# An attention and bilinear FFN kernel: the first FFN step with four a-parts ahead of four b-parts

## The chip, the cores and the metric

One core of a Trainium2 chip runs the program. The metric is the device time of one execution in microseconds (us). The span in a profile, from the first to the last instruction, is about 1.8 us less.

## The reference, cut to what matters

```
q, k, v: (4, 8, 768, 64) fp32;  w_a, w_b: (512, 1536);  w_out: (1536, 512)
x   = lightning attention(q, k, v, lam)     # blockwise, with a decayed state, as (3072, 512)
out = ((x @ w_a) * (x @ w_b)) @ w_out       # (3072, 512) fp32
```

## The kernel before

The kernel works on 24 units of 128 rows. The first four are prepared at once, and the FFN is then done in groups of units with the attention of later units hidden between its matmuls. The first group runs its FFN while the weights are still coming in: w_a and w_b arrive as six chunks each of 256 columns (512 KB in fp32) and are cast to bf16, a0 on GpSimd, b0 and the other w_a chunks on VectorE, the other w_b chunks on ScalarE. A chunk feeds two "parts" of 128 columns with four matmuls each (the very first part is done in two cuts of rows, so it has eight). I call the chunks a0, b0, a1, b1 and so on.

```
pending = []                                  # order of the weight loads
for c in range(len(W_CHUNKS)):
    pending += [("a", c), ("b", c)]
...
# ffn(), first group
for c, w in enumerate(W_CHUNKS):
    fs = range(w_off[c] // 128, w_off[c + 1] // 128)
    a_sbs = [a_part(f, ...) for f in fs]      # 4 matmuls; ScalarE copies the result out
    if c + 1 < len(W_CHUNKS):
        cast_w("a", c + 1, "dve")
    for f, a_sb in zip(fs, a_sbs):
        b_part(f, xT, gt, a_sb, ab)           # 4 matmuls; VectorE multiplies a by b
        hook(f)                               # f = 0: state of unit 3, kvd matmuls + a state copy
    if c + 1 < len(W_CHUNKS):
        cast_w("b", c + 1, "act")
...
cast_w("a", 0, "pool")                        # ahead of the FFN
cast_w("b", 0, "dve")
```

## Time and profile before

| | before |
|---|---|
| median of the three runs first given | 233.59 us (233.25 to 234.13) |
| span of the profiled execution (a further one, which took 234.34 us) | 232.6 us |
| TensorE busy | 96% |
| longest TensorE wait after 18 us | 0.79 us, for the cast of a1 |

A timeline line reads: start, length, engine, source line, operation, output and inputs, count, and in brackets the idle time before it with what ended it. Some matmul records are missing from a trace, so x11 can stand for twelve. A cast that waited for a transfer starts 0.02 to 0.05 us after the transfer has landed in these traces, so its start serves as the landing.

### The profile page before, as it was taken

What the parts mean: (1) busy time and instruction counts of PE and PEld (TensorE: products, weight loads), DVE (VectorE), ACT (ScalarE), POOL (GpSimd) and SP (SyncE); (2) the same over time, 40 slices, a digit from 0 to 9 for tenths busy, and PEclk for the clock granted to TensorE, in tenths of its full rate; (3) what the DMA queues carried; (4) which work ended last, traced back from release to release, by engine and by line L of the source; (5) the groups of instructions that cost most, each with busy time, mean ns of one, the idle gap of its engine ahead of it and who ended that gap; (6) DMA issues with size and microseconds to landing.
All of it is one profiled execution on the core that took longest, in us unless ns stands there. A gap on an engine that the chain in (4) does not pass through costs nothing.

```text
span 232.6 us, 4506 instructions
## 1 busy us (share of the span) xinstructions
PE 223.8 (96%) x1756; PEld 124.8 (54%) x1779; DVE 116.4 (50%) x204; ACT 91.0 (39%) x172; POOL 50.4 (22%) x65
## 2 busy tenths in 40 slices
PE   7798999999999999999999999999999999999994
PEld 2574444449698654454544454544454544444493
DVE  1894666646479745684335474235483323332050
ACT  3683764056564342332233332333332333332261
POOL 6061000245655243333300543000300000000000
PEclk9999999999999999999999999999999999999999
DMA  4999999999999999999959997229300220000311
GB/s 150 300 264 351 348 361 298 268 209 193 204 223 164 214 188 221 217 171 205 333 192 206 213 181 129 93 92 202 69 3 0 90 93 0 1 0 10 128 45 48
DMA packets 96453, 38.84 MB, mean 167 GB/s; under 512 B 83376, under 2 KB 91952, under 8 KB 96432
## 3 DMA queue, kind: packets, MB, share of 16 engines
q1 hardware_dynamic: 96288, 38.54, 72.8%
q8 instruction: 14, 0.23, 0.4%
q14 instruction: 7, 0.06, 0.1%
q10 hardware_dynamic: 144, 0.00, 0.0%
HBM read 28.32 MB, written 6.29 MB: 149 GB/s over the span
## 4 chain that ended last, share of the span: by engine, by line
PE 87%; DMA 6%; SPq 3%; ACT 1%; issue 1%; DVE 0%
PE a_ps L434 26%; PE b_ps L434 26%; PE op L467 26%; DMA wst<-in_moe_w_a_dram 4%; SPq L128 3%; PE kq L308 2%; PE o_ps L350 2%; DMA q<-in_q_dram 2%; PE o_ps L340 2%; PE kvd L364 1%; PE tps L294 1%; SPq L149 1%; ACT o_kept L458 1%; DVE wa_sb L164 0%; PE kvd L385 0%
## 5 line engine op out<-in xcount | busy, mean ns | idle before, releaser
L447 DVE TENSOR_TENSOR ab<-a_sb,b_ps 128x512 bf16<-128x512 bf16 (+2 forms) x96 | 52.5, 552 | 76.7 <-PE b_ps L434 55.2
L434 PE MATMUL a_ps<-xT,wa_sb 128*128 128x512 bf16 (+3 forms) x378 | 76.5, 323 | 1.7 <-DVE wa_sb L164 0.8
L434 PE MATMUL b_ps<-xT,wb_sb 128*128 128x512 bf16 (+2 forms) x383 | 77.0, 326 | 0.1
L442 ACT CAST a_sb<-a_ps 128x512 bf16<-128x512 f32 (+2 forms) x96 | 45.5, 481 | 61.5 <-PE a_ps L434 58.1
L467 PE MATMUL op<-wo_sb,ab 128*128 128x512 bf16 (+2 forms) x300 | 64.2, 362 | 0.8 <-issue 0.3
L434 PEld LDWEIGHTS <-wb_sb 128*128 128x128 bf16 x384 | 34.4, 98 | 28.9 <-ACT wb_sb L159 0.5
L434 PEld LDWEIGHTS <-wa_sb 128*128 128x128 bf16 x388 | 33.9, 98 | 29.6 <-DVE wa_sb L164 1.3
L467 PEld LDWEIGHTS <-ab 128*128 128x128 bf16 x312 | 28.8, 98 | 29.9
L325 DVE TENSOR_TENSOR m<-kq,lotri 128x512 bf16<-128x512 f32 x47 | 29.3, 682 | 17.2 <-PE kq L308 17.1
L257 POOL TENSOR_TENSOR qk<-kf,lp_k 128x512 bf16<-128x512 f32 x18 | 19.0, 1056 | 75.1 <-PE a_ps L434 38.1
L262 POOL TENSOR_TENSOR qk<-qf,lp_q 128x512 bf16<-128x512 f32 x20 | 21.8, 1092 | 24.1 <-DMA qf<-in_q_dram 24.1
L462 ACT COPY o_sb<-op 128x512 f32<-128x512 f32 (+2 forms) x19 | 10.3, 541 | 34.0 <-PE op L467 34.0
L357 ACT CAST xT<-o_ps 128x512 bf16<-128x512 f32 x22 | 12.0, 590 | 18.1 <-PE o_ps L350 17.5
L396 DVE TENSOR_TENSOR st<-kvd,bdiag 128x512 bf16<-128x512 f32 x18 | 12.3, 683 | 3.9 <-PE kvd L364 3.2
L271 DVE CAST vb<-vf 128x512 bf16<-128x512 f32 x17 | 9.5, 560 | 0.0
L296 ACT COPY qkT<-tps 128x1024 bf16<-128x1024 bf16 x5 | 5.1, 1012 | 9.9 <-PE tps L294 9.9
L197 PE MATMUL idle<-idle_sb 128*128 128x128 bf16 (+1 forms) x31 | 7.1, 371 | 1.3 <-DVE idle_sb L192 1.3
L350 PE MATMUL o_ps<-m,vb 128*64 128x128 bf16 x192 | 7.9, 222 | 0.0
L271 POOL CAST vb<-vf 128x512 bf16<-128x512 f32 x7 | 4.4, 631 | 13.6 <-DMA vf<-in_v_dram 13.6
L159 ACT CAST wb_sb<-wst 128x1024 bf16<-128x1024 f32 x5 | 5.2, 1046 | 4.7 <-DMA wst<-in_moe_w_b_dram 4.7
L340 PEld LDWEIGHTS <-st 128*128 128x128 bf16 x80 | 5.4, 98 | 2.8
L308 PE MATMUL kq<-qkT 64*128 64x128 bf16 x160 | 6.6, 218 | 0.0
(57 smaller groups left out, 87.4 us busy)
## 6 DMA issues: line engine op xcount, KB each, us to landing
vf<-in_v_dram SPq DMA_DIRECT2D x24, 256.0 KB, 4.9
qf<-in_q_dram SPq DMA_DIRECT2D x20, 256.0 KB, 4.6
kf<-in_k_dram SPq DMA_DIRECT2D x20, 256.0 KB, 4.7
out_dram<-o_sb SPq DMA_DIRECT2D x16, 256.0 KB, 2.0
wst<-in_moe_w_a_dram SPq DMA_DIRECT2D x6, 512.0 KB, 8.8
wst<-in_moe_w_b_dram SPq DMA_DIRECT2D x6, 512.0 KB, 8.8
wst<-in_moe_w_out_dram SPq DMA_DIRECT2D x6, 512.0 KB, 8.6
out_dram<-o_kept SPq DMA_DIRECT2D x7, 256.0 KB, 2.8
```

Source lines behind the costliest of these rows:

```text
L257: eng_of(eng).tensor_mul(qk[:, 1], raw.pop((u, "k")), lp_k[:, u % NB].to_broadcast([128, H, D]))
L262: eng_of(eng).tensor_mul(U[u]["qk"][:, 0], raw.pop((u, "q")), lp_q[:, u % NB].to_broadcast([128, H, D]))
L271: eng_of(eng).tensor_copy(vb, vf)
L308: nc.tensor.matmul(kq[i][:, hp, :], lhsT=d["kT"][p, hp, :], rhs=d["qT"][p, hp, :], start=True, stop=True, skip_group_check=True)
L325: nc.vector.tensor_mul(m, kq[i], lotri_bc)
L350: nc.tensor.matmul(d["o"][p, hp, :], lhsT=d["vb"][:, 2 * hp + i, :], rhs=d["m"](i, hp), start=(first and hp == 0), stop=True, skip_group_c ...
L357: nc.scalar.copy(xT[:, :, col:col + BLK], o_ps)
L396: nc.vector.tensor_mul(st[:].rearrange("p hp i d -> p hp (i d)"), ps[:].rearrange("p hp i d -> p hp (i d)"), bdiag_bc)
L434: nc.tensor.matmul(ps[:, lo:hi], lhsT=w_sb[:, s, f * 128:(f + 1) * 128], rhs=xT[:, s, lo:hi], start=(s == 0), stop=(s == KS - 1), skip_gro ...
L442: nc.scalar.copy(a_sb[:, :gt], ps[:, :gt])
L447: nc.vector.tensor_mul(ab[:, f, :gt], a_sb[:, :gt], ps[:, :gt])
L467: nc.tensor.matmul(op[:, lo:hi], lhsT=ab[:, f, t * 128:(t + 1) * 128], rhs=wo_sb[:, f, lo:hi], start=(f == 0), stop=(f == FC - 1))
```

## The change

The intent is to give TensorE two blocks of a-parts while the first w_b chunk is still on its way: the loads become a0, a1, b0, b1, a2, ..., and the first step does four a-parts and then four b-parts.

```diff
+W_STEPS = ((0, 1), (2,), (3,), (4,), (5,))
-    a_pool = ctx.enter_context(tc.tile_pool(name="a", bufs=3))
+    a_pool = ctx.enter_context(tc.tile_pool(name="a", bufs=5))
-    for c in range(len(W_CHUNKS)):
-        pending += [("a", c), ("b", c)]
+    for cs in W_STEPS:
+        pending += [("a", c) for c in cs] + [("b", c) for c in cs]
...
-            for c, w in enumerate(W_CHUNKS):
-                fs = range(w_off[c] // 128, w_off[c + 1] // 128)
+            for i, cs in enumerate(W_STEPS):
+                nxt = W_STEPS[i + 1][0] if i + 1 < len(W_STEPS) else None
+                fs = range(w_off[cs[0]] // 128, w_off[cs[-1] + 1] // 128)
                 a_sbs = [a_part(...) for f in fs]
-                if c + 1 < len(W_CHUNKS):
-                    cast_w("a", c + 1, "dve")
-                for f, a_sb in zip(fs, a_sbs):
+                if i == 0:
+                    cast_w("b", cs[1], "act")
+                elif nxt:
+                    cast_w("a", nxt, "dve")
+                for n_f, (f, a_sb) in enumerate(zip(fs, a_sbs)):
                     b_part(f, xT, gt, a_sb, ab)
                     hook(f)
-                if c + 1 < len(W_CHUNKS):
-                    cast_w("b", c + 1, "act")
+                    if i == 0 and n_f == 1:
+                        cast_w("a", nxt, "dve")
+                if nxt:
+                    cast_w("b", nxt, "act")
...
+    cast_w("a", 1, "dve")
     cast_w("b", 0, "dve")
```

## The prediction

> **What bounds the kernel now.** I read the page's busy shares first, then the waits of TensorE, then the timeline of the stretch that the change touches.
>
> From the page, the totals and the head of the chain that ended last:
>
> ```profile
> PE 223.8 (96%) x1756; PEld 124.8 (54%) x1779; DVE 116.4 (50%) x204; ACT 91.0 (39%) x172; POOL 50.4 (22%) x65
> ...
> PE 87%; DMA 6%; SPq 3%; ACT 1%; issue 1%; DVE 0%
> ```
>
> TensorE is busy 223.8 of 232.6 us, and the chain that sets the end is TensorE for 87% of the span. A change of order that leaves the matmuls alone can gain only what TensorE waits. All its waits are these (engine, line, what it waited for, us in total, times, longest):
>
> ```profile
> PE idle L197 <- DVE idle_sb L192: 1.3, 1, 1.3
> PE tk L541 <- DVE scratch L532: 1.0, 2, 0.8
> PE a_ps L434 <- DVE wa_sb L164: 0.8, 1, 0.8
> PE a_ps L434 <- ACT xT L357: 0.4, 2, 0.2
> ```
>
> The third line is the one in reach of this change: 0.8 us, once, before the second w_a chunk. Here is where it comes from, in the timelines of TensorE and VectorE from 18 to 28 us (start, length, engine, line, operation, count, idle time before):
>
> ```profile
> 18.16 1.90 PE L434 MATMUL a_ps<-xT,wa_sb 128*128 128x384 bf16 x11 [0.23 <-ACT xT L357]
> 19.90 1.03 PE L434 MATMUL b_ps<-xT,wb_sb 128*128 128x512 bf16 x4
> 20.76 0.39 PE L364 MATMUL kvd<-vb,scratch 128*128 128x128 bf16 x4
> 20.98 1.03 PE L434 MATMUL b_ps<-xT,wb_sb 128*128 128x512 bf16 x4
> 22.80 1.90 PE L434 MATMUL a_ps<-xT,wa_sb 128*128 128x512 bf16 x8 [0.79 <-DVE wa_sb L164]
> 24.66 1.90 PE L434 MATMUL b_ps<-xT,wb_sb 128*128 128x512 bf16 x8
> 26.40 1.89 PE L434 MATMUL a_ps<-xT,wa_sb 128*128 128x512 bf16 x8
> ```
>
> ```profile
> 19.12 0.69 DVE L164 CAST wb_sb<-wst 128x1024 bf16<-128x1024 f32 x1 [0.68 <-DMA wst<-in_moe_w_b_dram]
> 22.05 0.69 DVE L164 CAST wa_sb<-wst 128x1024 bf16<-128x1024 f32 x1 [2.23 <-DMA wst<-in_moe_w_a_dram]
> 22.66 0.68 DVE L447 TENSOR_TENSOR ab<-a_sb,b_ps 128x512 bf16<-128x512 bf16 x1
> 23.25 0.68 DVE L396 TENSOR_TENSOR st<-kvd,bdiag 128x512 bf16<-128x512 f32 x1
> 23.85 0.68 DVE L447 TENSOR_TENSOR ab<-a_sb,b_ps 128x512 bf16<-128x512 bf16 x1
> 25.06 0.69 DVE L164 CAST wa_sb<-wst 128x1024 bf16<-128x1024 f32 x1 [0.53 <-DMA wst<-in_moe_w_a_dram]
> ```
>
> ```profile
> 23.56 1.04 ACT L159 CAST wb_sb<-wst 128x1024 bf16<-128x1024 f32 x1 [2.88 <-DMA wst<-in_moe_w_b_dram]
> ```
>
> Call the 512 KB weight chunks a0, b0, a1, b1, a2 and so on. Where a cast's engine sat idle until a transfer, the cast's start is the landing. The second chunk in the queue landed at 19.12 us, the third at 22.05, the fourth at 23.56, the fifth at 25.06: a step of 2.9 us and from then on 1.5 us each. TensorE needs 1.73 us for a chunk (24.66 to 26.40 is 1.74; eight matmuls of 0.216). So TensorE runs dry once, at the third chunk, and the supply stays ahead afterwards. Everything after 26.4 us is TensorE at full rate.
>
> **What the Trainium skill says.** "DMA: Bandwidth & Descriptors", section "Why a DMA increments its semaphore by 16 and not by 1": a transfer counts as landed only when each of the engines that share it has finished. That fits a third chunk 2.9 us behind the second although the windows view has 351 GB/s moving from 17.9 to 22.8 us, at which 512 KB take 1.5 us: the rest was later chunks in flight. "TensorE: Matmul & The Clock Gate", section "Part 1: The HAM clock gate (the "warmup" mystery)": the array falls to half clock after an idle window of about 3.4 us. The wait here is 0.79 us and the granted clock is 1.00 from 17.9 to 52.4 us, which agrees. The same part calls VectorE and ScalarE strict FIFOs; the order of casts, products and evacuations on each engine is therefore that of the program, and the trace shows them so.
>
> **The change, part by part.** I compared the programs of the two kernels on each engine.
>
> 1. *What stays.* TensorE has 3560 rows in both, VectorE 145, and after the first two chunks of the first FFN step the order is the same. No work is removed.
>
> 2. *Transfers.* The queue becomes a0, a1, b0, b1, a2, ...: only the second and third chunk swap. Both are 128x1024 fp32, so I let the landings stay with the place in the queue: a1 at 19.12, b0 at 22.05, b1 at 23.56, a2 at 25.06.
>
> 3. *TensorE up to the third chunk.* a0 runs as before. a1 is cast by VectorE from 19.12 to 19.81 (0.69) and starts at about 19.9, where b0 started. It takes 1.73 us, to 21.6. Then b0 is wanted: landing 22.05, VectorE cast 0.69, and the start at 22.80, exactly where a1 started before. Two chunks' work is available before the third lands, in either order; the order of the names doesn't change that. The wait grows from 0.79 to about 1.2 us, because piece V of unit 3 (the four kvd matmuls, 0.22 us, from 20.76 to 20.98) hangs on the first b-part and has left this gap.
>
> 4. *From 22.80 on.* b0 now carries the kvd matmuls: 1.73 + 0.22 = 1.95, so b1 could start at 24.75. Its cast on ScalarE is ready at 23.56 + 1.04 = 24.60. Before, TensorE was ready at 22.80 + 1.73 = 24.53 and started b1 at 24.66, so 0.13 us of waiting was paid there and now isn't. Net: 24.75 against 24.66, +0.09 us.
>
> 5. *VectorE before a2.* The a2 cast now stands behind the first two products and the state copy. First product: its fourth matmul starts at 22.80 + 3 x 0.216 = 23.45, lasts 0.38, and a product follows its last matmul by 0.11 (26.67 against 24.66 + 1.90): 23.94. With starts 0.60 apart when queued (22.66, 23.25, 23.85): state copy 24.54, second product 25.14, a2 cast about 25.76 to 26.45. From a cast's end to a matmul is 0.06 (22.74 to 22.80), so a2 can start at 26.51; TensorE is ready at 24.75 + 1.73 = 26.48. Before, a2 started at 26.40. The cast's slack of 0.65 us is used up, but only just: +0.11 us in all.
>
> 6. *Buffers.* Eight parts are in hand, not four. The PSUM bank of a part is asked for again seven parts later, some 6 us on, and a_sb gets five buffers; neither makes a new wait. The b2 cast (landing 26.56, ready 27.60) is wanted at 28.2 as before.
>
> Sum: 0.22 (kvd matmuls moved onto the path) - 0.13 (wait for b1 gone) + 0.02 (wait for the a2 cast) = +0.11 us. All that follows is TensorE at full rate and is shifted by it: 233.59 + 0.11 = 233.7 us.
>
> **The rivals.** (a) *The gap closes.* This is the hope behind such a change: both a-chunks ahead give TensorE work while b is on its way. It holds only if the third chunk lands earlier than before. For it: the 2.9 us step is irregular, so it may belong to that one transfer or moment; against it: two chunks are consumed before the third is needed in both orders. At most the wait and the fourth chunk's wait go: 0.8 + 0.1 us, 232.7. (b) *VectorE becomes the bound at a2.* Step 5 leaves nothing to spare: if the a2 cast slips by one VectorE operation (0.6 us) TensorE stops again at 26.4, and the time is about 234.3. For it: three operations and a cast in 2.5 us; against it: a2 lands at 25.06 and the durations are very steady (687 to 694 ns for the five w_a casts). (c) *The longer wait of 1.2 us costs clock.* The skill's 3.4 us speaks against it; if it came, some 3 us at half rate would add about 1.5 us: 235.2.
>
> **Range and chances.** Three runs of before span 233.25 to 234.13, which is several times the effect. The range takes in most of rival (a) and all of (b), plus that spread: 233.0 to 234.4, with 233.7 in the middle. 2% is 4.7 us; nothing here reaches a fifth of that except (c), and not even it the whole. Faster by over 2%: 0.01; within 2%: 0.98; slower: 0.01.
>
> **What would show it right or wrong.** Right: the w_b cast of b0 on VectorE begins near 22 us after an idle stretch; TensorE's one wait there, now for the VectorE cast of wb_sb, is near 1.2 us and ends near 22.8; the kvd matmuls stand between the two halves of b0; no wait of over 0.1 us at b1 and a2. Wrong: b0 landing well before 22 us (then rival a, and step 2 is at fault), or a wait of some tenths at a2 for VectorE (rival b, step 5), or a granted clock below 1.00 after the wait (rival c).

## The result, and the profile after

The changed kernel took 234.41 us (median of 5, 234.06 to 234.88) against 233.81 us (median of 5, 233.25 to 234.29). The ratio is 1.0029, with a 95% interval of 1.0005 to 1.0052. The class "within 2%" was right; the time lies 0.01 us above the predicted range, and the difference of the medians is 0.6 us, not 0.11.

The page of the changed kernel, totals and head of the chain:

```profile
PE 225.6 (97%) x1779; PEld 124.8 (54%) x1779; DVE 116.4 (50%) x204; ACT 91.0 (39%) x172; POOL 50.1 (22%) x65
...
PE 90%; DMA 5%; SPq 2%; ACT 1%; POOL 0%; issue 0%
```

The balance is as before. The two TensorE totals can't be set against each other, because the trace of before holds 1756 matmul records and this one 1779, while both hold 1779 weight loads. Its timelines from 18 to 26 us, TensorE, GpSimd and VectorE:

```profile
18.67 3.64 PE L435 MATMUL a_ps<-xT,wa_sb 128*128 128x384 bf16 x20 [0.60 <-POOL wa_sb L162]
22.15 1.03 PE L435 MATMUL b_ps<-xT,wb_sb 128*128 128x512 bf16 x4
23.01 0.39 PE L365 MATMUL kvd<-vb,scratch 128*128 128x128 bf16 x4
23.23 2.75 PE L435 MATMUL b_ps<-xT,wb_sb 128*128 128x512 bf16 x12
25.92 1.90 PE L435 MATMUL a_ps<-xT,wa_sb 128*128 128x512 bf16 x8
```

```profile
18.00 0.61 POOL L162 CAST wa_sb<-wst 128x512 bf16<-128x512 f32 x1 [1.17 <-DMA wst<-in_moe_w_a_dram]
```

```profile
19.46 0.69 DVE L165 CAST wa_sb<-wst 128x1024 bf16<-128x1024 f32 x1 [0.87 <-DMA wst<-in_moe_w_a_dram]
20.96 0.69 DVE L165 CAST wb_sb<-wst 128x1024 bf16<-128x1024 f32 x1 [0.81 <-DMA wst<-in_moe_w_b_dram]
23.38 0.69 DVE L448 TENSOR_TENSOR ab<-a_sb,b_ps 128x512 bf16<-128x512 bf16 x1 [1.72 <-PE b_ps L435]
23.98 0.68 DVE L397 TENSOR_TENSOR st<-kvd,bdiag 128x512 bf16<-128x512 f32 x1
24.58 0.68 DVE L448 TENSOR_TENSOR ab<-a_sb,b_ps 128x512 bf16<-128x512 bf16 x1
25.18 0.68 DVE L165 CAST wa_sb<-wst 128x1024 bf16<-128x1024 f32 x1
```

Three things are to be seen. The wait at the third chunk is gone: b0 lands at 20.96 us, not at 22.05. In its place TensorE waits 0.60 us at the start, because a0 lands at 18.00 us instead of 17.20. (About 0.23 us of it is no loss: in the traces where a0 is on time TensorE stands that long for the copy of xT, as the first line of the prediction's timeline shows.) And the a2 cast starts without idle time behind the second product, as step 5 has it; the load of a2's weights then waited for it:

```profile
25.92 0.98 PEld L435 LDWEIGHTS <-wa_sb 128*128 128x128 bf16 x6 [0.42 <-DVE wa_sb L165]
```

One point does not fit a simple story. This profiled execution has a span of 232.3 us, less than the 232.6 us of the profile of before. One trace of each kernel doesn't stand for its kernel here, which is what the experiments are about.

### The profile page after: what moved, and what is told of

It is laid out like the page before. It is cut to its first block, busy times and chain, and to the rows that moved or that the text cites. A ratio compares the mean times of both kernels' runs of the same rounds, so it can differ in the third digit from the quotient of the medians.

```text
span 232.3 us, 4528 instructions
## 1 busy us (share of the span) xinstructions
PE 225.6 (97%) x1779; PEld 124.8 (54%) x1779; DVE 116.4 (50%) x204; ACT 91.0 (39%) x172; POOL 50.1 (22%) x65
## 4 chain that ended last, share of the span: by engine, by line
PE 90%; DMA 5%; SPq 2%; ACT 1%; POOL 0%; issue 0%
PE a_ps L435 27%; PE b_ps L435 27%; PE op L468 27%; DMA wst<-in_moe_w_a_dram 3%; PE kq L309 2%; PE o_ps L351 2%; SPq L129 2%; DMA q<-in_q_dram 2%; PE o_ps L341 2%; PE kvd L365 1%; PE tps L295 1%; ACT o_kept L459 1%; PE kvd L386 0%; POOL wa_sb L162 0%; ACT xT L358 0%
## 5 line engine op out<-in xcount | busy, mean ns | idle before, releaser
L468 PE MATMUL op<-wo_sb,ab 128*128 128x512 bf16 (+2 forms) x312 | 65.6, 363 | 0.0
L263 POOL TENSOR_TENSOR qk<-qf,lp_q 128x512 bf16<-128x512 f32 x20 | 21.8, 1090 | 22.8 <-DMA qf<-in_q_dram 22.8
L351 PEld LDWEIGHTS <-vb 128*64 128x64 bf16 x192 | 5.8, 109 | 1.4
```

Of the source, the lines that this page charges most:

```text
L263: eng_of(eng).tensor_mul(U[u]["qk"][:, 0], raw.pop((u, "q")), lp_q[:, u % NB].to_broadcast([128, H, D]))
L351: nc.tensor.matmul(d["o"][p, hp, :], lhsT=d["vb"][:, 2 * hp + i, :], rhs=d["m"](i, hp), start=(first and hp == 0), stop=True, skip_group_c ...
L468: nc.tensor.matmul(op[:, lo:hi], lhsT=ab[:, f, t * 128:(t + 1) * 128], rhs=wo_sb[:, f, lo:hi], start=(f == 0), stop=(f == FC - 1))
```

## The experiments

Eighteen runs were made. My theory at first (order): what counts is the order of work on TensorE and VectorE after 22 us. Rivals: the order of the loads sets when a0 lands (transfers), or the executions scatter and one trace of each says little (scatter). Three numbers were read from each trace: the start of a0's matmuls, the time from there to the first a2 matmul, and what is lost after that.

### Both kernels again, and two repairs of the order

r_before and r_after are the two kernels unchanged.

> The kernel before, unchanged, against itself. All theories: ratio 1.000 within about 0.002. It gives a second trace of before. If the third chunk's late landing (2.9 us behind the second) belongs to that one execution, the step is 1.5 us here, TensorE has no 0.8 us wait for the cast of wa_sb, and the first a2 matmul starts near 25.8 us instead of 26.40. If it belongs to the order of loads a0, b0, a1, the step is again near 2.9 us.

> The changed kernel, unchanged: ratio 1.003 as measured on the first occasion if the loss is real, 1.000 if it was the scatter of executions. Second trace: under the theory that the order of loads sets the landings (both a-chunks of one tensor first), the first chunk lands near 18.0 us again and TensorE waits some 0.6 us for the GpSimd cast of a0; under the scatter theory the landing of a0 moves by several tenths.

v3_early moves the four kvd matmuls and their state copy between the halves of the a1 block:

```diff
+                    if i == 0 and f == 2:
+                        hook(-1)          # V of unit 3, its PLAN slot 0 made -1
```

> Changed kernel with the four kvd matmuls and the state copy of unit 3 put between the two halves of the a1 block, so neither lies between b0 and the a2 cast. Order theory (my step 4 and 5): the loss goes, ratio to before 1.000 or 0.1 us under it, and no wait for the VectorE cast before a2. Transfer theory or start theory: stays where the changed kernel is, about 1.003, at most 0.1 us better.

a2_first casts a2 right after the first product of b0:

```diff
+                    if i == 0 and n_f == 0:
+                        cast_w("a", nxt, "dve")
                     hook(f)
-                    if i == 0 and n_f == 1:
-                        cast_w("a", nxt, "dve")
```

> Changed kernel with the VectorE cast of a2 issued straight after the first product of b0, ahead of the state copy and the second product. Order theory with VectorE at a2 as the cause (rival b of the prediction): the loss goes, about 1.000 to 1.001. If only the 0.1 us of the a2 wait hangs on it: 0.1 us better than the changed kernel. Transfer or start theory: same as the changed kernel.

| run | median us | ratio to before (95%) | a0 starts | a0 to a2 | span |
|---|---|---|---|---|---|
| r_before | 233.73 | 1.0006 (0.996 to 1.005) | 18.10 | 7.15 | 231.5 |
| r_after | 234.08 | 0.9997 (0.997 to 1.002) | 18.13 | 7.25 | 232.3 |
| v3_early | 233.62 | 0.9982 (0.995 to 1.001) | 18.74 | 7.22 | 232.2 |
| a2_first | 234.25 | 1.0011 (0.998 to 1.004) | 18.26 | 7.14 | 232.3 |

The loss of the first occasion did not repeat: the mean of r_after is that of before. Before itself went from 233.12 to 235.03 us in its 11 runs here. No order shows a gain or loss in the times. The traces say more. This is before in r_before, TensorE and one line of VectorE:

```profile
18.10 1.90 PE L434 MATMUL a_ps<-xT,wa_sb 128*128 128x384 bf16 x12 [0.23 <-ACT xT L357]
...
21.78 1.89 PE L434 MATMUL a_ps<-xT,wa_sb 128*128 128x512 bf16 x8
23.51 1.90 PE L434 MATMUL b_ps<-xT,wb_sb 128*128 128x512 bf16 x8
25.25 1.89 PE L434 MATMUL a_ps<-xT,wa_sb 128*128 128x512 bf16 x8
```

```profile
20.92 0.69 DVE L164 CAST wa_sb<-wst 128x1024 bf16<-128x1024 f32 x1 [1.76 <-DMA wst<-in_moe_w_a_dram]
```

The third chunk landed at 20.92 us, 2.5 us behind the second (18.46), and TensorE never stood for it. The 0.79 us wait that my prediction was built around is not a property of the kernel before; it came in one execution and not in the next. With no wait, a0 to a2 takes 7.15 us: four blocks of 1.73 and the kvd matmuls of 0.22 make 7.14. The changed kernel takes 7.25 in each of its five traces, and a2_first brings it back to 7.14 (best, below, which has the same edit, to 7.17):

```profile
18.26 3.62 PE L435 MATMUL a_ps<-xT,wa_sb 128*128 128x384 bf16 x20 [0.23 <-ACT xT L358]
...
25.40 1.89 PE L435 MATMUL a_ps<-xT,wa_sb 128*128 128x512 bf16 x8
```

So the a2 cast behind two more VectorE operations costs 0.10 us, and this part of the order theory stands. v3_early gained only 0.03 us, because with the kvd matmuls gone from b0 TensorE reached b1 some 0.1 us before its ScalarE cast was done.

r_after lost another 0.6 us far from the change, near 74 us. Here are its TensorE wait, its VectorE and its GpSimd lines:

```profile
PE kvd L365 <- DVE st L397: 0.6, 1, 0.6
```

```profile
72.52 1.12 DVE L272 CAST vb<-vf 128x512 bf16<-128x512 f32 x1
...
73.89 0.68 DVE L397 TENSOR_TENSOR st<-kvd,bdiag 128x512 bf16<-128x512 f32 x1
```

```profile
72.31 1.04 POOL L263 TENSOR_TENSOR qk<-qf,lp_q 128x512 bf16<-128x512 f32 x1
```

And the same VectorE cast and GpSimd product in r_before:

```profile
72.38 0.42 DVE L271 CAST vb<-vf 128x512 bf16<-128x512 f32 x1
```

```profile
71.20 1.04 POOL L262 TENSOR_TENSOR qk<-qf,lp_q 128x512 bf16<-128x512 f32 x1
```

In r_before GpSimd was done at 72.24 and the cast took 0.42 us. In r_after GpSimd ran until 73.35 and the cast took 1.12 us, the state copy behind it came late, and TensorE waited 0.57 us for it. The Trainium skill, "SBUF — State Buffer", section "Who interferes with whom", says that a VectorE instruction in a two-port mode, which a cast can enter, and GpSimd share a port pair, and that the one that starts second blocks for the whole of the other's instruction. These traces agree: 0.42 us alone, 1.12 us beside GpSimd. In seven traces (r_after, a2_first, a_look2, b_look2, r_after2, rows_plus and a_rows36) the cast started 0.3 to 0.9 us before the end of the product, and in all seven it ended 0.28 us after that end, having taken 0.56 to 1.14 us. It strikes in either kernel: in b_look2, a trace of before, the cast took 0.72 us and TensorE waited 0.17 us. What brings the two together was not tested; the GpSimd products wait for the transfers of k or for TensorE, so their place can move.

### Which loads make a0 late?

In all four traces of the changed load order a0 landed 5.8 to 6.3 us after its issue, in both of before after 5.4. Three runs test the transfers theory. loads_only is before with the new order of loads, loads_old is the changed kernel with the old one:

```diff
 # loads_only, in the kernel before
-    for c in range(len(W_CHUNKS)):
-        pending += [("a", c), ("b", c)]
+    for cs in ((0, 1), (2,), (3,), (4,), (5,)):
+        pending += [("a", c) for c in cs] + [("b", c) for c in cs]
 # loads_old, in the changed kernel: the reverse
```

> Kernel before with only the order of the weight loads of the changed kernel (a0, a1, b0, b1, ...); its engines still want a0, b0, a1. Theory 'two a-chunks in a row delay a0': a0 lands about 6.0 us after its issue (5.8 to 6.3 in the four traces of kernels with that order) instead of 5.4 (both traces of before). Scatter theory: anything from 5.4 to 6.3. The time is disturbed by design: b0 is third in the queue, TensorE stands from the end of a0 (19.9) to about 21.7, so some 1.5 to 2 us more than before.

> Changed kernel with only the order of the weight loads of before (a0, b0, a1, b1, ...). Theory 'two a-chunks in a row delay a0': a0 lands about 5.4 us after its issue and TensorE starts a0 with no wait for the GpSimd cast. Scatter theory: anything from 5.4 to 6.3. Time disturbed by design: a1 is third, 1.5 to 2 us more than before.

far takes a3 in place of a1 as the second chunk: `W_STEPS = ((0, 3), (1,), (2,), (4,), (5,))`, with the cast and the range of parts to match.

> Changed kernel whose second a-chunk is a3 (columns 768 to 1023) in place of a1 (columns 256 to 511), so the two first transfers read places in the rows of w_a that are 3 KB apart and not side by side. If a0 is late because its neighbour in memory is read at the same time: a0 lands 5.4 us after its issue. If it is late because both chunks come from the same tensor, or for any reason of the queue: about 6.0 us as in the changed kernel. Time: like the changed kernel, or 0.2 to 0.5 us better in the first case.

The landing of a0 after its issue was 6.2 us in loads_only, 6.6 in loads_old and 6.3 in far. The transfers theory is contradicted by loads_old, which has the old order and the latest a0 of the three. In far a0 was late too, though the first two chunks are not neighbours in memory. The times were 235.0 and 235.56 us for the two mixed orders, 1.3 and 1.8 us over before, as a chunk wanted second and loaded third must cost; far was like before (ratio 0.9998, 0.998 to 1.002).

What the late chunks have in common lies in the transfers themselves. A transfer completes in 16 shares, and the trace has the time of each. The list of transfers also has a queue, q8 "instruction", with 14 packets of 16 KB in a span. One of them falls near the first chunks. The DMA view of three short stretches, each about a packet, of before (18.4 to 18.7 us), after (14.9 to 15.1) and rows_plus, a run told below (11.4 to 11.6); columns are packets, MB and share of the 16 engines, where the packet's whole time is set against the short stretch (0.217 x 16 x 0.3 us = 1.04 us):

```profile
q8 instruction: 1, 0.02, 21.7%
```

```profile
q8 instruction: 1, 0.02, 34.8%
```

```profile
q8 instruction: 1, 0.02, 34.4%
```

Such a packet takes about 1.1 us (0.93 to 1.48 in the traces near the chunks), while 512 KB take 1.5 us on all 16 engines together. The trace kept here doesn't tell which engine a packet is on; that it is one of those that carry the chunks is my inference. The traces of the two kernels, unchanged, in the order of the packet:

| trace | packet at us | a0 lands | last share behind the median (8th) share: first chunk, third chunk | TensorE wait for the a0 cast | wait for the third chunk |
|---|---|---|---|---|---|
| b_look3 (before) | 14.6 | 18.5 | 2.1, 2.1 | 1.17 | 0 |
| after | 15.0 | 18.0 | 1.3, 1.2 | 0.60 | 0 |
| r_after2 (after) | 15.3 | 18.2 | 1.7, 1.6 | 1.00 | 0 |
| a_look (after) | 15.7 | 18.9 | 2.6, 2.6 | 1.64 | 0 |
| r_after (after) | 17.2 | 17.5 | 1.1, 1.5 | 0.25 | 0 |
| r_before (before) | 17.3 | 17.0 | 0.6, 1.6 | 0 | 0 |
| a_look2 (after) | 17.4 | 17.9 | 1.2, 0.9 | 0.28 | 0 |
| b_look (before) | 17.5 | 17.3 | 0.9, 1.7 | 0 | 0 |
| before | 18.5 | 17.2 | 0.7, 2.6 | 0 | 0.79 |
| b_look2 (before) | 18.6 | 17.2 | 0.6, 2.4 | 0 | 0.62 |

With the packet at 15.7 us or earlier, the last share of a0 is 1.3 to 2.6 us behind the median one and TensorE waits 0.6 to 1.6 us for a0. With the packet at 17.2 us or later a0's last share is 0.6 to 1.2 us behind and TensorE waits 0.3 us at most, of which 0.23 us would be spent on xT anyway. At 18.5 us it is the third chunk that is late, and TensorE waits there. This holds for both kernels, and in the seven traces of the variants above and below that leave the warm-up alone: packet at 14.2 to 15.1 us and a wait of 0.6 to 1.0 us before a0 in v3_early, loads_only, loads_old, far and best, packet at 17.5 and 18.3 us and no such wait in a2_first and before_vb. A share that has fallen behind stays behind: in before the last share is 2.5 us late for each of the third to sixth chunks, in b_look3 2.1 us for all six, as if one engine had lost that time once. It is an association over seventeen traces, as an experiment can't take the packet away.

### Moving the packet, and a version with the repairs

rows_plus is before with 13 warm-up matmuls of 512 columns made 52 of 128, `warm(13, 512)` to `warm(52, 128)`.

> Kernel before, with the 13 warm-up matmuls of 512 columns made 52 of 128 columns: 78 more TensorE instructions before the first real one, the same work. If the 16 KB packet is the fetch of TensorE's instruction stream, it moves earlier by the time of some 78 instructions, to about 11 to 13 us (from 14.2 to 18.6 in the ten traces so far); then a0 is always late, TensorE waits 0.5 us or more for its cast, and there is no wait at the third chunk beyond it. If it is not TensorE's, it stays between 14 and 18.6. Time: within 0.5 us of before.

The packet came at 11.52 us and the next one at 21.62 (27.5 to 28.9 in the ten traces above). Both moved up by several us, so it is TensorE's instruction stream that is fetched. The Trainium skill, "Runtime: NRT & Kernel Launch", section "Instruction fetch mechanics", gives blocks of 16 KiB for 256 instructions. By this figure 14 blocks are an estimated 3584 instructions, and the trace of the changed kernel holds 1779 matmuls and 1779 weight loads, 3558 together, which agrees. The expectation that a0 is then always late was wrong: it landed at 17.53 us, TensorE did not wait for it, and a0 to a2 took 7.13 us. But the third v block landed at 14.75 us (14.35 in before) and a0 started at 18.57, so the time was 234.31 us (ratio 1.001, 0.9993 to 1.0027).

r_after2 is the changed kernel a third time.

> The changed kernel again. Fetch theory (new): one 16 KB packet of instructions, about 1.1 us long, falls between 14 and 18.6 us on one of the DMA engines that carry the chunks, and puts every chunk after it about 1 us back; before about 15.1 us it makes a0 late (landing near 18.0, TensorE wait 0.6 us), after about 17 us the third chunk and later ones. It falls in either place in both kernels, so the mean differs by the 0.1 us of the a2 cast only: ratio 1.000 to 1.001. Order-of-loads theory: ratio about 1.002 to 1.003 and a0 late in this trace too.

It took 234.29 us, ratio 1.0015 (0.9995 to 1.0035); the order-of-loads ratio of 1.002 to 1.003 is not excluded by the interval, but loads_old had spoken against that theory.

before_vb moves the VectorE cast of v of unit 10 behind the state copy of unit 7 near 72 us: in the plan, `(6, "P", 10)` becomes `(6, "PK", 10)` and, after `(7, "V", 7)`, `(7, "PV", 10)`.

> Kernel before with the VectorE cast of v of unit 10 moved behind the state copy of unit 7 (near 72 us). In two traces of the changed order that cast took 1.1 us in place of 0.42 while GpSimd worked on the next unit, and TensorE then waited 0.6 us for the state copy. If part of the executions of before lose 0.6 us there too, the mean falls by up to 0.3 us (ratio 0.9987 to 1.000); if before never does, ratio 1.000.

It gave 1.0011 (0.9986 to 1.0037): no gain that the scatter lets one see.

best has this edit and a2_first on the changed kernel, and the GpSimd cast of a0 in four pieces.

> Changed kernel with the a2 cast straight after the first product, the v cast of unit 10 behind the state copy of unit 7, and the GpSimd cast of a0 in four pieces, so that TensorE can start on half of the first weights. Order theory: 0.1 us from the a2 cast. Fetch theory: up to 0.3 us more where a0 is late, 0.6 us where the GpSimd collision near 72 us would have come. Together ratio 0.998 to 0.999 to before; if none of these matters, 1.000.

Its median was 233.82 us against 234.06, ratio 0.9982 with an interval of 0.9963 to 1.0001. It may be a little faster than both kernels, but it isn't shown. Its traced execution had the packet at 15.1 us, and TensorE waited 0.89 us for a0 all the same.

b_rows36 and a_rows36 put 36 more TensorE instructions in the warm-up (`warm(7, 512)` and `warm(24, 128)`) and the v cast behind the state copy, in before and in the changed kernel.

> Kernel before with 36 more TensorE instructions in the warm-up (same work) and the v cast of unit 10 behind the state copy. Fetch theory: the 16 KB packet moves to about 12 to 14 us, ahead of the chunks, where only the v loads are in flight, and the chunks land 1.5 us apart with none late: a0 starts near 18.1 with no wait for its cast, a2 starts 7.15 us later, near 25.3, and the time is that of the best executions of before, 233.2 to 233.5, ratio 0.997 to 0.998. If the lateness has another cause: like before, 1.000.

> The same two edits on the changed kernel. With the fetch and the GpSimd collision out of the way in both, the order is all that is left: a0 to a2 takes 7.25 us in place of 7.15 (the a2 cast on VectorE), so 0.1 us more than b_rows36, 0.0 to 0.2. Order-of-loads theory: 0.4 us or more over b_rows36, with a0 landing late.

The packet did move, to 12.9 and 13.0 us, but the chunks were not on time: a0 landed at 17.97 in b_rows36 and TensorE waited 0.48 us; in a_rows36 the second chunk came late and TensorE waited 0.82 us for it, and 0.46 us more for b2. The times were 233.96 and 234.38 us, ratios 1.0007 (0.998 to 1.003) and 1.0025 (1.000 to 1.005). With the packet moved, the last share of the late chunk was still 1.3 and 1.8 us behind the median, so the packet's place alone doesn't decide. The attempt to get it out of the way failed, and the 0.4 us between the two is not the pure price of the order that I wanted to measure.

### Does the change move the packet?

b_look, b_look2 and b_look3 are before, a_look and a_look2 the changed kernel, each for one more trace.

> Kernel before, for its trace: where does the 16 KB packet fall? If each execution draws it, some traces of before have it before 15.3 us with a0 late (so far 0 of 3 with before's own order of loads, 1 of 1 with the changed loads). If the program sets it, before has it at 17 to 18.6 us again. Time near 233.9.

> The changed kernel, for its trace: so far the packet fell at 15.0, 17.2 and 15.3 us. Drawn by each execution: either place. Time near 234.2; a0 start 18.1 if late, 18.6 to 18.9 if early.

> Kernel before, for its trace. Drawn by each execution alike in both kernels: the 16 KB packet before 15.7 us in about half of the traces. Shifted by the change: 17.3 to 18.6 us again, as in all four traces of before's own orders (18.5, 17.3, 18.3, 17.5), and a0 lands by 17.4 us.

> The kernel before once more, for one more trace; the same two expectations as for b_look2: packet before 15.7 us half of the time if drawn, 17.3 to 18.6 us if the change is what shifts it.

> The changed kernel, for its trace. Shifted by the change: the packet before 15.7 us (so in 3 of its 4 traces, the fourth at 17.2) and a0 landing at 18 us or later, with a TensorE wait of 0.6 us or more for its cast. Drawn alike: either.

The start of a0 in b_look3 (before) and in a_look (changed):

```profile
19.21 1.91 PE L434 MATMUL a_ps<-xT,wa_sb 128*128 128x384 bf16 x11 [1.17 <-POOL wa_sb L161]
```

```profile
19.61 3.64 PE L435 MATMUL a_ps<-xT,wa_sb 128*128 128x384 bf16 x19 [1.64 <-POOL wa_sb L162]
```

The kernel before has the early packet and the late a0 too, in one of five traces; the changed kernel has it in three of five. So the change isn't needed for it. Whether it makes it more frequent can't be told from ten traces. Counting the variants with an unchanged warm-up too, the packet was early in 8 of 11 traces of kernels with the change or a part of it and in 1 of 6 of before and before_vb. That was counted after the fact, and a split as uneven comes by chance in about 4% of cases: a hint that the change shifts the packet, not a proof. The medians were 233.53, 234.44 and 234.28 us for before and 234.25 and 234.24 for the changed kernel, of two runs each.

## Why the prediction was right or wrong

**All runs together.** The changed kernel ran 21 times, before 64 times, on five occasions on which both ran and one more with before alone. The medians are 234.19 and 233.92 us. Taking the difference of the means within each occasion (0.67, -0.01, 0.30, 0.54 and -0.03 us, one run of before at 236.69 left out) and weighting by the changed kernel's runs gives 0.29 us, with two standard errors of about 0.25 from the spreads of 0.43 and 0.50 us. So the change costs something between almost nothing and 0.5 us. The 0.6 us of the first occasion was at the high end, and the 0.11 us predicted is inside.

**Step by step.**

- *Steps 1 and 6*, what stays and the buffers: right as far as seen; there is no wait for a PSUM bank or an a_sb buffer in any trace of the change. Five a_sb buffers alone were not tried. The 3560 and 145 rows of step 1 stand in no trace; the traces of both kernels hold 1779 weight loads of TensorE and 204 VectorE instructions.
- *Step 2, "I let the landings stay with the place in the queue"*: this is the step that failed. I read 17.20, 19.12 and 22.05 us from one execution and took them for the kernel. That execution took 234.34 us, 0.75 us more than the median of 233.59 to which I added my 0.11. Over five traces of before, a0 landed at 17.0 to 18.5 us and the third chunk at 20.9 to 22.1; in the changed kernel at 17.5 to 18.9 and 20.8 to 21.9.
- *Step 3*, a wait of 1.2 us for b0 ending at 22.8: wrong in all five traces, through step 2. The 1.2 was mis-sized too: 0.79 us counts from the end of the last matmul and 1.2 from where the next one could start; by the measure of the 0.79 it is 0.79 + 0.22 = 1.0. In no trace of the changed kernel did TensorE stand for the third chunk. It stood before a0 instead, 0.25 to 1.64 us (0.23 of it in any case), which the prediction left out.
- *Steps 4 and 5*: the sum fits the constant part by luck, its terms were wrong. The constant part of the loss measured 0.10 us, 7.25 in place of 7.15 us from a0 to a2. It is the wait for the a2 cast alone, for which I had 0.02: I let the first product begin 1.14 us after b0's first matmul (22.80 to 23.94), and it began 1.23 us after it (22.15 to 23.38 in the trace shown, 1.23 in all five). The 0.22 for the kvd matmuls is paid in both kernels when TensorE has no gap to hide them in, and the wait of 0.13 for b1 belongs to the late third chunk. These two terms came from the gap and are not in the measured 0.10.
- *Rival (a)*, the gap closes: it did, but in before as well, by the draw of the execution. It is worth 1.09 us (8.24 us from a0 to a2 in the trace of before, 7.15 without it), not the 0.9 I added up from idle times. *Rival (b)*: 0.1 us of it came. *Rival (c)*: the granted clock stayed at 0.997 or more in all runs of the change.
- *The range*: taken from three runs of before (0.9 us apart). The 64 runs told more: 233.12 to 235.03, and one of 236.69.

**Where the time of the change goes.** In the five traces of each kernel the mean span is 232.26 us before and 232.54 after, 0.28 more. It splits into the start of a0, 18.39 against 18.77 (+0.38); a0 to a2, 7.56 against 7.25 (-0.31, because two traces of before stood for the third chunk); and the rest, 206.30 against 206.51 (+0.21). Of the rest, 0.14 us is the wait near 74 us (0.57 us in r_after and 0.29 in a_look2 against 0.17 in b_look2, as means over five traces); the other 0.07 was not traced. Shown as a fixed cost of the change is the 0.10 us at a2. The start of a0 goes with the place of the instruction packet and the wait near 74 us with the VectorE and GpSimd overlap, in the traces of both kernels. Whether the change shifts their odds, and so what it costs in the mean, stays open.

## What to carry to other kernels

Count the blocks that are ready before the next transfer lands, in both orders: here there are two in each, so the new order by itself buys no time (an argument; no run isolates it). Before building a prediction on a wait that one trace shows once, take a second and third trace of the same kernel: a wait that hangs on the last of 16 shares of a transfer may be the execution's and not the program's. A change that aims at less than the scatter between executions (here 2 us) can be judged by the steady intervals in the traces, such as 7.15 against 7.25 us, long before the times can tell.

## What the Trainium skill lacked or had wrong

- "Runtime: NRT & Kernel Launch", section "Instruction fetch mechanics", calls the cost of crossing a 16 KiB boundary mostly hidden. No page has a figure for what a fetch costs the data transfers beside it. Here a packet of 16 KB took 0.93 to 1.48 us near the weight chunks, and in those of the ten traces where it came at 15.7 us or earlier the last share of the first chunk was 1.3 to 2.6 us behind the median share, against 0.6 to 1.2 us where it came later (an association, as said above).
- "DMA: Bandwidth & Descriptors" has no figure for how far the 16 shares of one transfer lie apart; here the last one was 0.6 to 2.6 us behind the median share of a 512 KB transfer that takes 1.5 us in steady flow.
- "SBUF — State Buffer", section "Who interferes with whom", was right and gives no durations: the VectorE cast of 128x512 took 0.42 us alone and up to 1.14 us beside a GpSimd product, and when blocked it ended 0.28 us after the product.
